# Sorted block attention into four weighted experts: the experts' weights of two chunks are spread over the partitions by GpSimd instead of by transfers, with 69 first dummy matmuls instead of 84

## The chip, the core and the metric

The kernel runs on one core of a Trainium2 chip. The metric is the device time of one execution in microseconds (us). Engines: PE multiplies matrices (PEld is its weight load), DVE is the vector engine, ACT the scalar engine, POOL is GpSimd, SP only issues transfers (DMA).

## What is computed

For each of 4 x 8 heads an 8 x 8 matrix is normalized over rows and columns five times. It mixes the 8 blocks of 96 keys and of 96 values. Each block of 96 queries attends to the mixed block at its place. The heads' results side by side are 3072 tokens x of width 512, which go through four experts; each expert's result counts with a weight p that depends on the token and the expert:

```python
p = domain_probs / (domain_probs.sum(-1, keepdims=True) + 1e-09)
for e in range(E):                       # 4 experts
    h = np.maximum(x @ w1[e], 0.0)       # 512 -> 1024
    out += p[:, e:e + 1] * (h @ w2[e])   # 1024 -> 512
```

## The kernel before

The order of the instructions on each engine is the order in which the program is written (manual_schedule): nothing is moved by a scheduler. Each engine works through its own list; semaphores make it wait for others.

**Start.** SP fetches the 8 x 8 matrices (L77) and the domain probabilities (L170, L171). PE runs `warm(84)` (L307), 84 matmuls on a constant tile that nobody reads. ACT and DVE take turns in the five normalization rounds (L309 to L327); after the last one `sn` is spread out (L330) and PE begins its real work with L342. Between rounds, `spread_weights` (L244) computes p on DVE, one step at a time. When p is done, SP writes its first 32 partitions, which hold batch 0's tokens, to a DRAM tile `p_dram` laid out expert by token (L256), and the rest after that (L258).

**Batch 0's attention, then its chunks.** Attention of batch 0 is done by the `h_` functions, in small steps between which expert 0's first layer (`group0`, L704) and second layer (`second_layer0`, L741) are put. Tokens are then handled in chunks of 256, three in a batch. `chunk_first(b, c, es, ...)` (L805) computes for each expert e of `es` the hidden values h: 2 groups of 16 matmuls (L815) into a PSUM tile of which there are two, and for each group one DVE instruction (L821) that takes max(h, 0), times the token's weight p for that expert, into `Hb`. Since tokens lie along the free axis there, p has to lie in the same row in all 128 partitions. That is what the tile `pb` is: 4 experts x 256 tokens, the same in each partition. Batch 0's expert 0 is handled otherwise, so its chunks need experts 1 to 3 only. `pb` has one buffer; the next chunk's weights can be written when the last L821 of the chunk is done.

**How pb is filled.** `load_p` (L226) is one transfer on SP's queue that reads a row of `p_dram` and writes it to all 128 partitions (512 KB for four experts). It is called for chunk (0, 0) right after L256 (L257), and for every next chunk in `chunk` (L847, L851). `load_p_one` (L238) fetches one expert's row of chunk (0, 1), 128 KB, into a part of tile `Tt[3]` (named T in the profile), for expert 1 of that chunk, which is computed early (call at L1506, use at L1516).

**POOL's list** holds all weight transfers (their descriptors are made by POOL: 0.7 to 0.9 us an issue), and its order matters here: `load_w1(1)`, the halves of `w1` of expert 2 (L1456), `load_w2(1)` and `load_w2(2)` (both issued at L146), `load_w1(3)` (L139), half of expert 3's `w2` (L1475), then four products that build mixing matrices for batch 1 (L372, L364 in `builds(1)`), then batch 1's queries (L126), values and keys (L113) with the other half of expert 3's `w2` among them. Before each issue POOL waits until the transfer that was issued eight before has landed.

**A chunk's second layer** (`chunk`, L834) is a sum of products of half blocks (a Strassen-like scheme). For chunk (0, 0) the steps are f1 (L950), f2 (L955), f3 and so on; between them some adds are POOL's (`gtt`: L953, L970, L971, L974, L995). POOL's list also has the query transfers of the next batch in between (L126). SP's list there: a transpose of queries (L413), pb of the next chunk (L230), six transfers of mixed values (L405), stores of the result (L876), more transposes.

**The end.** The last chunks (`last_first`, `last_second`) multiply again in seven products instead of eight (L1153, L1296); there POOL multiplies by p in L1166, 48 times in the last three pairs of chunks.

Of the kernel before, what the change touches and what calls it, by code (L numbers as in the profile page):

```python
# [2 lines left out]

# [7 lines left out]
F32 = mybir.dt.float32  # L11
# [7 lines left out]
def kernel(  # L19
# [11 lines left out]
    nc = tc.nc  # L31

    B, H, S, D = q.shape
# [4 lines left out]
    E = moe_w1.shape[0]  # L38
    FF = moe_w1.shape[2]
    P = 128  # L40
# [22 lines left out]
    moe = ctx.enter_context(tc.tile_pool(name="moe", bufs=2))  # L63
# [8 lines left out]
    def psm(shape, dtype, name):  # L72
        return psM.tile(shape, dtype, tag="ps", name=name)
# [46 lines left out]
    def load_queries(b, heads=range(H)):  # L120

        if (b, "q") not in natural:
            natural[(b, "q")] = arena[:, ds(4 * NW, NQ)].rearrange("p (n t h d) -> p n t h d", n=NPB, t=R, h=2)
        t = natural[(b, "q")]
        for h in heads:
            nc.gpsimd.dma_start(t[:, h // 2, :, h % 2, :], q[b, h].rearrange("(t p) d -> p t d", p=P))  # L126
# [16 lines left out]
    def load_w2(e, parts=1):  # L143
        n = NFC // parts
        for i in range(parts):
            nc.gpsimd.dma_start(  # L146
                w2sb[e][:, ds(i * n, n)], moe_w2[e].rearrange("(fc p) d -> p fc d", p=P)[:, ds(i * n, n)]
            )
# [71 lines left out]
    p_dram = dramp.tile([E, N], F32, name="p_dram")  # L220
# [2 lines left out]

    pbs = {}

    def load_p(b, c, es=range(E), pb=None):  # L226
        if pb is None:
            pb = moe.tile([P, E, 2 * P], F32, name=f"pb_{b}_{c}", tag="pb", bufs=1)
        n = len(es)
        nc.sync.dma_start(  # L230
            pb[:, ds(es[0], n)],
            p_dram[ds(es[0], n), ds(b * S + 2 * c * P, 2 * P)].rearrange("(o e) x -> o e x", o=1).broadcast_to(
                [P, n, 2 * P]
            ),
        )
        return pb

    def load_p_one(b, c, e):  # L238

        pb = Tt[3].rearrange("p a f x -> p (a f x)")[:, 0:4 * P].bitcast(F32)  # L240
        nc.sync.dma_start(pb, p_dram[ds(e, 1), ds(b * S + 2 * c * P, 2 * P)].broadcast_to([P, 2 * P]))
        return pb

    def spread_weights():  # L244

        nc.vector.tensor_reduce(p_den, p_in, AX.X, ALU.add)
        yield
        nc.vector.tensor_scalar(out=p_den, in0=p_den, scalar1=1e-9, scalar2=None, op0=ALU.add)
        yield
        nc.vector.reciprocal(p_den, p_den)  # L250
        yield
        nc.vector.tensor_tensor(
            p_out.rearrange("p e t -> p t e"), p_in, p_den.broadcast_to([P, NT, E]), ALU.mult
        )
        p_rows = p_dram.rearrange("e (p t) -> p e t", t=NT)
        nc.sync.dma_start(p_rows[0:S_P], p_out[0:S_P])  # L256
        pbs[(0, 0)] = load_p(0, 0)  # L257
        nc.sync.dma_start(p_rows[S_P:P], p_out[S_P:P])  # L258
        yield

# [11 lines left out]
    def warm(n):  # L272
        ps = psM.tile([P, 4, P], F32, tag="ps", name=f"ps_w_{state['n']}")
        state["n"] += 1
        for m in range(n):
            nc.tensor.matmul(ps[:, m % 4, :], dummy, dummy, start=True, stop=True)
# [27 lines left out]
    srow = const.tile([GH, NB, 1], F32, name="srow")  # L304
    scol = const.tile([GH, NB, 1], F32, name="scol")
    sn16 = const.tile([GH, NB, NB, CP], F16, name="sn16")
    warm(84)  # L307
    p_steps = spread_weights()
    for it in range(5):  # L309
        nc.scalar.activation(sn[:], sn[:], AF.Exp, bias=0.0, scale=1.0)  # L310
# [371 lines left out]
    def h0(fc):  # L682

        return Hflat[:, ds((0 if fc < KH else 3) * NFC * 2 * P + (fc % KH) * HS, HS)]
# [50 lines left out]
    def second_layer0(hf, slot):  # L735
        for t in range(R // 2):
            col = (R // 2) * hf + t
            po = psm([P, 2, 512], F32, f"ps_o_{col}")
            ps = po[:, 0, 0:Dm]
            for fc in range(NFC):  # L740
                nc.tensor.matmul(  # L741
                    ps, h0(fc)[:, ds(t * P, P)], w2sb[0][:, fc, :],
                    start=(fc == 0), stop=(fc == NFC - 1),
                )
                if fc == KH - 1:
                    slot()
            oaccs[col] = room[:, col - 2] if col > 1 else moeo.tile([P, Dm], F32, name=f"oacc_{col}", tag="oacc")
            nc.vector.tensor_scalar(
                out=oaccs[col][:], in0=ps, scalar1=p_sb[:, col], scalar2=None, op0=ALU.mult
            )  # L750
            slot()
# [53 lines left out]
    def chunk_first(b, c, es, first, slot, weights=None):  # L805

        xT = xTs[b].rearrange("p k i x -> p k (i x)")
        if weights is None:
            weights = lambda e: pbs[(b, c)][:, ds(e, 1), :]
        for e in es:  # L810
            for g in range(2):
                ps = psm([P, 4, 2 * P], F32, f"ps_h_{b}_{c}_{e}_{g}")
                for f in range(4):
                    for kc in range(NKC):
                        nc.tensor.matmul(  # L815
                            ps[:, f, :],
                            w1sb[e][:, kc, ds((4 * g + f) * P, P)],
                            xT[:, kc, ds(2 * c * P, 2 * P)],
                            start=(kc == 0), stop=(kc == NKC - 1),
                        )  # L820
                nc.vector.scalar_tensor_tensor(  # L821
                    out=Hb[:, homes.get(e, e), ds(4 * g, 4), :], in0=ps[:], scalar=0.0,
                    op0=ALU.max, in1=weights(e).broadcast_to([P, 4, 2 * P]), op1=ALU.mult,
                )
                late = e == E - 1 or b > c
                if e > first and (g or not late):
                    two = (2,) if b or c else (2, 3)
                    if b > c or (b, c, e) == (0, R // 2 - 1, E - 2):
                        two = ()
                    for w in (1, *two) if late else ((1,), two)[g]:  # L830
                        h_sums(e - 1, w)
                slot()

    def chunk(b, c, slot, done=()):  # L834

        es = list(range(E)) if b else list(range(1, E))
# [7 lines left out]
                h_sums(e, 2)  # L844
        nxt = (b, c + 1) if c + 1 < R // 2 else (b + 1, 0)
        first = int(nxt[0] == 0)
        pbs[nxt] = load_p(*nxt, range(first, first + 1))  # L847
        rest = lambda: load_p(*nxt, range(first + 1, E), pbs[nxt])
        late = b == c == 1
        if not late:  # L850
            rest()  # L851

        blk = lambda kh, tok: (lambda e, f: Hb[:, homes.get(e, e), kh * KH + f, ds(tok * P, P)])
        sm = lambda n: (lambda e, f: Sb[:, n, e, ds(f * P, P)])
# [1 line left out]
        def product(n, lhs, rhs, pool=psm):  # L856
            ps = pool([P, DH], F32, f"ps_{n}_{b}_{c}")
            for e in es:
                for f in range(KH):
                    nc.tensor.matmul(  # L860
                        ps[:], lhs(e, f), Ts[e][rhs][:, f, :],
                        start=(e == es[0] and f == 0), stop=(e == E - 1 and f == KH - 1),
                    )
            return ps[:]
# [7 lines left out]
        o = out[ds(b * S, S), :].rearrange("(t p) d -> p t d", p=P)  # L872
# [82 lines left out]
        def f2():  # L955
            tt(oa1, product("p2", blk(1, 0), "b21"), oa1, ALU.add)
            slot()
# [22 lines left out]
            h_sums(e, 4)  # L980
        next(steps)
        f2()
        next(steps)
        h_sums(E - 1, 3)
        f3()
# [483 lines left out]
            build_PI(nc.gpsimd, n, "k")  # L1469

    load_w2(1)
    load_w2(2)
    load_w1(3)
    def load_w2_part(e, d):
# [22 lines left out]
                f(*args)  # L1497

    second_layer0(0, next_stages)
    load_queries(1, range(2))  # L1500
    load_natural(1, "v", 0, 2, lambda: load_w2_part(3, DH))
    load_natural(1, "k", 0, 2)
    load_natural(1, "v", 1)
    load_natural(1, "k", 1)
    chunk_first(0, 0, [1, 2], 1, next_stages)
    pb_1 = load_p_one(0, 1, 1)  # L1506
    h_sums(1, 4)
    for w in range(1, 5):
        h_sums(2, w)
# [3 lines left out]
    second_layer0(1, lambda: next(sums2, None))  # L1513
    sums0 = weight_sums(0, nc.vector)
    homes[1] = 0
    chunk_first(0, 1, [1], 1, next_stages, lambda e: pb_1.rearrange("p (o x) -> p o x", o=1))  # L1516
    homes.clear()


    for g in range(G0 + 1):  # L1520
        b, c = divmod(g, R // 2)
# [5 lines left out]
        def slot(b=b, c=c, at=at):  # L1527
            here = (c, at[0])
            for cc, n, f, *args in PLANS[b]:
                if (cc, n) == here:  # L1530
                    f(*args)
            if b:
                for cc, n, *args in PLAN_A:
                    if (cc, n) == here:
                        input_sums(*args)
                if here == (1, 12):
                    token_sums(G0, slice(0, 3))
                if here == (2, 0):
                    token_sums(G0, slice(3, 4))
            at[0] += 1  # L1540
# [6 lines left out]
    for g in range(G0 + 1, GN, 2):  # L1547
        last_second(g, last_first(g))
        last_second(g + 1, upper=True)
# [1 line left out]
_INS = ['q', 'k', 'v', 'sort_net', 'moe_domain_probs', 'moe_w1', 'moe_w2']  # L1551
_OUTS = [((3072, 512), 'float32')]
# [25 lines left out]
```

## Time and profile before

| | |
|---|---|
| three runs | 358.37, 358.61, 359.99 us (median 358.61) |
| the profiled execution | 358.21 us |
| its span, first to last instruction | 356.3 us |
| PE busy | 350.4 us (98%) |
| DVE, ACT, POOL busy | 277.5, 170.1, 137.6 us |
| PE's granted clock | 1.0 throughout |

A line of a timeline reads: start in us, duration in us, engine, line of the kernel, operation, written tile <- read tiles, shape, count, and in brackets how long the engine was idle just before and what ended that. A line of the waits reads: engine and line that waited <- engine and line waited for: us in total, times, longest. In the list of transfers the last number of a line is the median of the us from issue to landing. In a table by stretches (start:end in us) the columns are the length of the stretch, then busy us and count by engine, the clock of PE, the share of the DMA engines, GB/s.

### The profile page before, as it was taken

Reading aid. Unit: us, or ns where it says so; the run is one execution under the profiler, and the core shown is the slowest. Engines: PE = TensorE matmul, PEld = TensorE weight load, DVE = VectorE, ACT = ScalarE, POOL = GpSimd, SP = SyncE. Lnnn points to the kernel's source line nnn. Section 1 sums busy time; section 2 is a strip of 40 time slices with the busy share of each in tenths; the row PEclk is TensorE's granted clock in tenths of the full one; section 3 lists DMA queues with packets and bytes.
Section 4 is the critical chain, followed back from the end, with each engine's and each line's share of the span. In section 5 each row is a group of like instructions: output and inputs, shape, how many; then the busy total and the mean of one; then the engine's idle time right before and its main releaser. Section 6 shows DMA issues by size and latency. Waiting matters only on the chain.

```text
span 356.3 us, 9511 instructions
## 1 busy us (share of the span) xinstructions
PE 350.4 (98%) x3948; PEld 305.5 (86%) x3948; DVE 277.5 (78%) x555; ACT 170.1 (48%) x302; POOL 137.6 (39%) x154
## 2 busy tenths in 40 slices
PE   8899999999999999999999999999999999999996
PEld 8686857888888888988899888888888888888886
DVE  5766787779798687778879988896678886588963
ACT  2653330452425445368847259830288611598301
POOL 8766112466022420000626318840068800188400
PEclk9999999999999999999999999999999999999999
DMA  8999999999999999743995410005200014100021
GB/s 104 203 205 230 212 209 194 207 195 167 195 180 166 195 116 203 138 88 44 180 205 91 107 74 0 2 1 136 78 26 3 2 37 141 62 0 2 0 75 46
DMA packets 74762, 40.26 MB, mean 113 GB/s; under 512 B 41568, under 2 KB 70496, under 8 KB 74720
## 3 DMA queue, kind: packets, MB, share of 16 engines
q0 software_dynamic: 38720, 19.93, 43.2%
q1 hardware_dynamic: 35856, 19.67, 27.2%
q8 instruction: 31, 0.51, 0.6%
q14 instruction: 11, 0.09, 0.1%
q10 hardware_dynamic: 144, 0.07, 0.1%
HBM read 41.88 MB, written 6.34 MB: 135 GB/s over the span
## 4 chain that ended last, share of the span: by engine, by line
PE 95%; DVE 3%; issue 0%; DMA 0%; ACT 0%; DVEq 0%
PE ps_h L815 18%; PE ps_Q L1296 18%; PE ps_p L799 12%; PE ps_X L1153 10%; PE ps_Z L1153 7%; PE ps_Q L1153 7%; PE ps_Z L1296 6%; PE ps_h L704 3%; PE ps_o L741 3%; PE ps_p L860 3%; PE ps_a L479 2%; PE ps_s L444 2%; PE ps_k L425 1%; PE ps_v L391 1%; PE ps_mv L521 1%; PE ps_a L593 0%
## 5 line engine op out<-in xcount | busy, mean ns | idle before, releaser
L815 PE MATMUL ps_h<-xT,w 128*128 128x256 f16 x576 | 67.5, 273 | 0.0
L815 PEld LDWEIGHTS <-w 128*128 128x128 f16 x576 | 55.2, 98 | 7.3
L821 DVE SCALAR_TENSOR_TENSOR Hb<-ps_h,pb 128x1024 f16<-128x1024 f32 x34 | 41.5, 1223 | 17.8 <-PE ps_h L815 17.6
L1153 PEld LDWEIGHTS <-w 128*128 128x128 f16 x480 | 43.6, 98 | 4.7
L1166 POOL TENSOR_TENSOR arena<-tmp,pb 128x512 f16<-128x512 f32 x12 | 15.2, 1276 | 65.7 <-PE ps_Z L1153 49.8
L1296 PEld LDWEIGHTS <-Hb 128*128 128x128 f16 x320 | 31.1, 98 | 3.5
L1165 ACT ACTIVATE tmp<-tmp 128x512 f32<-128x512 f32 x46 | 29.0, 632 | 3.9 <-DVE tmp L1203 3.9
L1296 PEld LDWEIGHTS <-Sb 128*128 128x128 f16 x304 | 28.2, 98 | 3.0
L1153 PEld LDWEIGHTS <-arena 128*128 128x128 f16 x312 | 27.7, 98 | 2.8
L451 ACT ACTIVATE ET<-ps_s 96x768 f16<-96x768 f32 x24 | 18.1, 802 | 25.2 <-PE ps_s L444 25.0
L434 ACT CAST kT<-ps_k 64x384 f16<-64x384 f32 x48 | 22.7, 473 | 13.3 <-PE ps_k L425 12.3
L126 POOL DMA_DIRECT2D arena<-in_q_dram x24 | 19.9, 842 | 20.8 <-DMA q_ring<-arena 17.7
L1153 PE MATMUL ps_X<-ET,arena 128*128 128x256 f16 x168 | 25.2, 272 | 0.0
L1296 PE MATMUL ps_Q<-w,Hb 128*128 128x256 f16 x192 | 24.6, 273 | 0.0
L799 PEld LDWEIGHTS <-Hb 128*128 128x128 f16 x232 | 21.9, 98 | 3.0
L1159 DVE SCALAR_TENSOR_TENSOR Hb<-ps_X,pb 128x512 f16<-128x512 f32 x27 | 18.7, 692 | 7.0 <-PE ps_X L1153 7.0
L1173 ACT COPY ps_X<-ps_Z 128x512 f32<-128x512 f32 x27 | 15.4, 571 | 17.8 <-PE ps_Z L1153 17.8
L1153 PE MATMUL ps_Z<-xT,w 128*128 128x256 f16 (+1 forms) x176 | 22.5, 258 | 0.0
L785 DVE TENSOR_TENSOR Sb<-Hb 128x512 f16<-128x512 f16 x33 | 20.6, 646 | 0.0
L1180 ACT COPY tmp<-ps_X 128x512 f32<-128x512 f32 x26 | 15.2, 586 | 9.2 <-PE ps_X L1153 6.6
L1159 DVE SCALAR_TENSOR_TENSOR Hb<-ps_Z,pb 128x512 f16<-128x512 f32 x27 | 18.4, 683 | 1.3 <-PE ps_Z L1153 1.3
L1203 DVE TENSOR_TENSOR tmp<-ps_Q,tmp 128x512 f32<-128x512 f32 x26 | 17.7, 683 | 0.8 <-PE ps_Q L1153 0.8
(270 smaller groups left out, 744.3 us busy)
## 6 DMA issues: line engine op xcount, KB each, us to landing
w<-in_moe_w_dram POOLq DMA_DIRECT2D x4, 1024.0 KB, 27.2
w<-in_moe_w_dram POOLq DMA_DIRECT2D x6, 512.0 KB, 19.7
arena<-in_k_dram POOLq DMA_DIRECT2D x7, 384.0 KB, 7.6
arena<-in_v_dram POOLq DMA_DIRECT2D x7, 384.0 KB, 8.1
vs<-arena SPq DMA_DIRECT2D x36, 66.0 KB, 5.3
arena<-in_q_dram POOLq DMA_DIRECT2D x24, 96.0 KB, 7.5
out_dram<-ob SPq DMA_DIRECT2D x9, 256.0 KB, 2.0
pb<-p_dram SPq DMA_DIRECT2D x4, 512.0 KB, 5.8
```

Source lines behind the costliest of these rows:

```text
L126: nc.gpsimd.dma_start(t[:, h // 2, :, h % 2, :], q[b, h].rearrange("(t p) d -> p t d", p=P))
L434: nc.scalar.copy(kT[ds(D * hh, D), r], pk[ds(D * r, D), hh].rearrange("p a (i c) -> p a i c", c=CP),)
L451: nc.scalar.activation(ETs[2 * (pr % 2) + hh][:, 0:S].rearrange("c (a x) -> c a x", a=2), pss[hh][0:BLK, :, 0:HS], AF.Exp, bias=0.0, scale ...
L785: tt(sm[0], blk(0, 1), blk(1, 1), ALU.add)
L799: nc.tensor.matmul(ps, lhs(e, f), Ts[e][rhs][:, f, :], start=(first and e == es[0] and f == 0), stop=(done and e == es[-1] and f == KH - 1 ...
L815: nc.tensor.matmul(ps[:, f, :], w1sb[e][:, kc, ds((4 * g + f) * P, P)], xT[:, kc, ds(2 * c * P, 2 * P)], start=(kc == 0), stop=(kc == NKC ...
L821: nc.vector.scalar_tensor_tensor(out=Hb[:, homes.get(e, e), ds(4 * g, 4), :], in0=ps[:], scalar=0.0, op0=ALU.max, in1=weights(e).broadcast ...
L1153: nc.tensor.matmul(dst[:, ds(f * cols, cols)], a[lhs][:, k, ds((f0 + f) * P, P)], t[rhs][:, k, :], start=(first and f == 0 and k == 0), st ...
L1159: nc.vector.scalar_tensor_tensor(out=home(i, j), in0=src.rearrange("p (f x) -> p f x", f=m), scalar=0.0, op0=ALU.max, in1=weight(j).broadc ...
L1165: nc.scalar.activation(src, src, AF.Relu, bias=0.0, scale=1.0)
L1203: tt(t12, Q, u2, ALU.add)
L1296: nc.tensor.matmul(ps, lhs(e, f), Ts[e][rhs][:, f, part], start=(first and e == 0 and f == 0), stop=(e == E - 1 and f == KH - 1), skip_gro ...
```

## The change

Three uses of transfers that write the same row to 128 partitions are replaced: chunk (0, 0), expert 1 of chunk (0, 1), and experts 2 and 3 of chunk (0, 1). Now a small transfer brings the rows to partition 0 (`load_rows`), and a GpSimd instruction copies partition 0 to all partitions (`spread`). [...] The row for `pb_1` is fetched and spread earlier in the lists than its transfer was: ahead of batch 1's query loads on POOL. The spread for chunk (0, 1) stands after f2 of chunk (0, 0) in the program, on POOL between L953 and the query loads. All other chunks use `load_p` as before. On PE, DVE and ACT nothing is moved; only 15 dummy matmuls with their weight loads are gone.

```diff
+    def pb_tile(b, c):
+        return moe.tile([P, E, 2 * P], F32, name=f"pb_{b}_{c}", tag="pb", bufs=1)
...
     def load_p_one(b, c, e):
         pb = Tt[3].rearrange("p a f x -> p (a f x)")[:, 0:4 * P].bitcast(F32)
-        nc.sync.dma_start(pb, p_dram[ds(e, 1), ds(b * S + 2 * c * P, 2 * P)].broadcast_to([P, 2 * P]))
+        pb = pb.rearrange("p (o x) -> p o x", o=1)
+        load_rows(pb, b, c, [e])
+        spread(pb)
         return pb
+
+    def load_rows(dst, b, c, es):
+        nc.sync.dma_start(
+            dst[0:1], p_dram[ds(es[0], len(es)), ds(b * S + 2 * c * P, 2 * P)].rearrange("(o e) x -> o e x", o=1)
+        )
+
+    def spread(dst):
+        nc.gpsimd.partition_broadcast(dst, dst[0:1])
...
         nc.sync.dma_start(p_rows[0:S_P], p_out[0:S_P])
-        pbs[(0, 0)] = load_p(0, 0)
+        pbs[(0, 0)] = pb_tile(0, 0)
+        load_rows(pbs[(0, 0)][:, 1:E], 0, 0, range(1, E))
         nc.sync.dma_start(p_rows[S_P:P], p_out[S_P:P])
...
-    warm(84)
+    warm(69)
...
-        pbs[nxt] = load_p(*nxt, range(first, first + 1))
-        rest = lambda: load_p(*nxt, range(first + 1, E), pbs[nxt])
         late = b == c == 1
-        if not late:
-            rest()
+        if nxt == (0, 1):
+            pbs[nxt] = pb_tile(*nxt)
+            load_rows(pbs[nxt][:, 2:E], *nxt, range(2, E))
+        else:
+            pbs[nxt] = load_p(*nxt, range(first, first + 1))
+            rest = lambda: load_p(*nxt, range(first + 1, E), pbs[nxt])
+            if not late:
+                rest()
...
         next(steps)
         f2()
+        spread(pbs[nxt][:, 2:E])
         next(steps)
...
     load_w2(1)
+    nc.gpsimd.load_library(library_config.all_libraries[10])
+    spread(pbs[(0, 0)][:, 1:E])
     load_w2(2)
...
     second_layer0(0, next_stages)
+    pb_1 = load_p_one(0, 1, 1)
     load_queries(1, range(2))
...
     chunk_first(0, 0, [1, 2], 1, next_stages)
-    pb_1 = load_p_one(0, 1, 1)
...
+    nc.gpsimd.load_library(library_config.standard)
```

More of the change, by code (lines that the diff above doesn't have):

```diff
@@ L5 @@
 import concourse.tile as tile
-from concourse import mybir
+from concourse import library_config, mybir
 from concourse.bass import ds
@@ L224 @@
     pbs = {}
+    def pb_tile(b, c):
+        return moe.tile([P, E, 2 * P], F32, name=f"pb_{b}_{c}", tag="pb", bufs=1)
     def load_p(b, c, es=range(E), pb=None):
         if pb is None:
-            pb = moe.tile([P, E, 2 * P], F32, name=f"pb_{b}_{c}", tag="pb", bufs=1)
+            pb = pb_tile(b, c)
         n = len(es)
@@ L1515 @@
     homes[1] = 0
-    chunk_first(0, 1, [1], 1, next_stages, lambda e: pb_1.rearrange("p (o x) -> p o x", o=1))
+    chunk_first(0, 1, [1], 1, next_stages, lambda e: pb_1)
     homes.clear()
```

## The prediction

> **What bounds the kernel now.** I read the page first (busy shares, then the chain that ended last), then the waits of TensorE alone, then POOL's and DVE's timelines around the changed lines, then the time to landing of the transfers issued there. Page:
>
> ```profile
> span 356.3 us, 9511 instructions
> ...
> PE 350.4 (98%) x3948; PEld 305.5 (86%) x3948; DVE 277.5 (78%) x555; ACT 170.1 (48%) x302; POOL 137.6 (39%) x154
> ...
> PE 95%; DVE 3%; issue 0%; DMA 0%; ACT 0%; DVEq 0%
> ```
>
> TensorE is on the chain for 95% of the span, DMA and POOL for nothing. A busy share alone could hide a PE that crawls, so the waits of the weight loads (PEld) over the whole run count more. Two of their lines:
>
> ```profile
> PEld L342 <- DVE sn L330: 1.4, 1, 1.4
> ...
> PEld L391 <- DMA arena<-in_v_dram: 0.2, 1, 0.2
> ```
>
> The first is the wait at 11.6 us for the end of the Sinkhorn rounds on ACT and DVE, which no edit touches. The second is all the time in the trace that PE waited for a transfer: 0.2 us. So whatever the change does to DMA, it has about 0.2 us to win in this trace, and the question is what it can break. What it touches, on POOL and DVE:
>
> ```profile
> 21.71 1.76 POOL L146 DMA_DIRECT2D w<-in_moe_w_dram  x2 [0.38 <-DMA w<-in_moe_w_dram]
> 23.50 0.75 POOL L139 DMA_DIRECT2D w<-in_moe_w_dram  x1
> 26.10 0.89 POOL L1475 DMA_DIRECT2D w<-in_moe_w_dram  x1 [1.86 <-DMA w<-in_moe_w_dram]
> 27.00 1.06 POOL L372 TENSOR_TENSOR arena<-maskv,Rs 128x512 f16<-128x512 f16 x1
> ...
> 40.88 0.90 POOL L1475 DMA_DIRECT2D w<-in_moe_w_dram  x1 [1.71 <-DMA w<-in_moe_w_dram]
> 47.35 0.70 POOL L113 DMA_DIRECT2D arena<-in_v_dram  x1 [5.58 <-DMA w<-in_moe_w_dram]
> ...
> 64.33 0.96 POOL L953 TENSOR_TENSOR oacc<-oacc,p 128x256 f32<-128x256 f32 x1 [2.83 <-ACT p L951]
> 65.25 1.69 POOL L126 DMA_DIRECT2D arena<-in_q_dram  x2
> 70.01 0.72 POOL L970 TENSOR_TENSOR oacc<-oacc,p 128x256 f32<-128x256 f32 x1 [3.07 <-ACT p L968]
> ```
>
> ```profile
> 38.79 1.23 DVE L821 SCALAR_TENSOR_TENSOR Hb<-ps_h,pb 128x1024 f16<-128x1024 f32 x1 [1.63 <-PE ps_h L815]
> ```
>
> ```profile
> pb<-p_dram SPq DMA_DIRECT2D x1, 512.0 KB, 10.4
> ...
> T<-p_dram SPq DMA_DIRECT2D x1, 128.0 KB, 12.6
> p_dram<-T SPq DMA_DIRECT2D x1, 36.0 KB, 12.2
> ```
>
> L821 at 38.79 us is the first reader of the spread weights; it waited for PE, not for them. The last fence is SP's transfers issued between 25 and 27 us, with the time to landing at the end of the line: the stretch is full of weight traffic, and even 36 KB took 12.2 us.
>
> **The change part by part.** All sums are made against the profiled execution: 358.2 us, span 356.3 and 1.9 around it. The median of the three runs, 358.6, lies 0.4 above it.
>
> *15 dummies fewer.* The first dummies by time, columns PE busy and count:
>
> ```profile
> 1.06:3.06 2.00, 2.00 (x19) 0.00 (x0) 1.00 0.16 31
> 3.06:5.06 2.00, 2.00 (x21) 0.00 (x0) 1.00 1.15 133
> 5.06:7.06 2.00, 2.00 (x39) 0.00 (x0) 1.00 1.17 127
> ```
>
> 105 ns each for the first 19, 51 ns in the third stretch. The 15 last cost 15 x 0.051 = 0.8 us, and the first 69 end near 6.5 us, after the speed doubled. PE then waits longer before L342 (1.2 us on its own row becomes 2.0): 0 on the path. If that cover were gone it would be a gain of at most 0.8.
>
> *Transfers removed.* 512 KB and 128 KB near 26 us, and 384 KB at 63.8 us, become rows of 3, 1 and 2 KB. The DMA moves 211 to 227 GB/s between 20 and 40 us, so 640 KB less lets the weights behind land about 3.0 us earlier. PE's wait for v goes: -0.2. Next is k at L425, which landed at 66.8 and is taken at 67.0; it would be early by the same 3 us. If the stream were not relieved (the change not doing what it says), this 0.2 alone is lost: 358.5.
>
> *Library load and first spread on POOL.* They stand between the two issues of L146, so POOL reaches them at 22.6. The trace has no real load. From below: the two configuration instructions of masks.py:199, 0.09 us each. [...] I take 10.4, the 512 KB transfer: the load ends at 33.0. The row of 3 KB is issued at 25.5 and lands in 1.5 (sn, 8 KB, idle DMA) to 12.2 us (36 KB); I take 5.5, the 12 KB write issued at 20.0: 31.0. The spread of 768 elements is 0.3 (a COPY of 128) to 1.9 us (1.28 of a TENSOR_TENSOR of 512 f32, times 1.5); I take 1.9. Done at 34.9, or 39.6 by the latest row; L821 wants it at 38.79, and PE goes on behind it, because its next group has a second PSUM buffer. Cost 0, slack 3.9.
>
> Behind the load on POOL wait three weight issues (2.5 us: to 37.4), four builds (4.1: 41.5), the second, smaller spread (0.6: 42.1; its reader L821 comes at 57.4), two query issues (43.8), v (44.5) and w2's second half, at 44.5 instead of 40.88. What hides it: the software queue holds a backlog. The w2 part issued at 21.71 landed 25.1 us later, at 46.8; the next only has to be in the queue by about 43.8 (3.0 us earlier than that landing), and it is at 34.9. At 47.35 POOL waited 5.58 us for a landing anyway, so there it is in step again. Without that backlog it would cost the whole 12 us.
>
> *Third spread.* On POOL after L953, waiting for a row issued at 63.8. Bounds 1.5 and 7.0 (128 KB there); 5.5 gives 69.3, the spread of 512 ends at 70.6, its reader L821 comes at 75.1. Queued behind it: two query issues (to 72.3 instead of 66.9), L970 and L971 (73.7), L995 (74.4), L974 (75.3), four query issues from 75.3 instead of 73.6. The first two queries landed after 10.7 us behind a backlog (76.8); issued late they take the 4.9 us of those issued at 70 to 75: 76.3, no later. The next two come 1.7 us later, and with them SP's queue: transposes, six vs transfers, the weights of the third chunk (85.2 to 86.9, 7.7 to landing: 94.6). Their L821 stands at 94.11, so DVE is 0.5 late; PE's third group there starts at 96.5 and needs that L821's end, 95.8. Cost 0.
>
> *Library at the end.* POOL's last TENSOR_TENSOR ends at 333.8 and PE's last matmul at 353.5: a load of 12.6 fits. 0.
>
> To cover the small slips in this I add 0.3: 358.2 - 0.2 + 0.3 = **358.3**.
>
> [...]
>
> **Rivals.**
> 1. *The load is slow; the kernel gets slower.* It decides from 14.3 us (22.6 + 14.3 + 1.9 = 38.8). For it: weights of 512 KB took 19.7 us to land (median of the six), and POOL can do nothing else meanwhile. Against it: SP's queue stayed under 12.7. At 19.7 the spread ends at 44.2, L821 at 45.4; PE's third group, at 41.1, waits 4.3: **362.5**.
> 2. *POOL is held at the third spread.* Decides from 6.8 us of landing: then the two queries pass 77.7, and PE's L444 at 86.08, whose operand landed at 85.2, waits. At 8.6 (the 256 KB there) 1.8 us: 360.0; at 12.2 about 5. Against it: two kilobytes.
> 3. *The new library's tensor_tensor is slower.* L1166 takes 1.27 us, twice in each step of 3.06 us. Up to 1.53 nothing is lost; at twice the time each of 24 steps loses 2.0: 407. The trace has no word for it.
> 4. *The clock drops in the longer wait at 11.6.* Half speed for 3.4 us would cost at most 1.7: 359.9. Against it: PEclk shows full clock, and 1.2 us of waiting did no harm. [...]
> 5. *Faster.* Unprofiled runs may wait for landings more than this trace does (one took 360.0). To pass 0.5% the gain must be 1.8 us, nine times the wait seen: 356.7.
>
> **Chances.** Forecast 0.52; slow load 0.20; third spread 0.13 (0.05 of it small); tensor_tensor 0.04; clock 0.03 (0.02 small); faster 0.08. Of a measurement of this kernel, 0.5% (1.8 us: 356.8 to 360.4) is about what can be told from no change. So faster 0.08, same 0.52 + 0.05 + 0.02 = 0.59, slower 0.20 + 0.08 + 0.04 + 0.01 = 0.33. The range runs from 357.4 (most of the gain left out) to 362.5 (slow load in, tensor_tensor and the worst rows out): about 0.8.
>
> **What would show it.** Right: PE's waits as before, without the one on v; POOL's spread before 38 us; L821 there still released by PE; the weights about 3 us earlier. Wrong: L821 released by POOL at 38.8 (rival 1); L444 near 86 waiting for q_ring (rival 2); L1166 far from 1.27 us (rival 3); matmuls after 11.6 at twice their length (rival 4). The forecast falls with any PE wait over 1.8 us that is not in the trace of before.

## The result, and the profile after

| | before | changed |
|---|---|---|
| median of 22 runs each | 358.37 us | 359.16 us |
| lowest to highest | 357.86 to 359.99 | 357.98 to 361.91 |
| ratio, 95% interval | | 1.0024 (1.0014 to 1.0034) |
| profiled execution, its span | 358.21, 356.3 | 360.12, 358.2 |

The changed kernel is 0.8 us (0.24%) slower. That is inside the range (357.4 to 362.5) and within the 0.5% that was called "same", but it is not the 0 that the sum gave: the interval leaves 1.0 out. The whole of it has to be explained by small things, so the experiments below count in tenths of a per cent.

In this kernel 14 lines were added ahead of the attention code: L821, L413, L405, L342, L479, L495 and L815 of before are L835, L427, L419, L356, L493, L509 and L829 here, and L230 is L233. The page of the changed kernel, its span, its busy shares and the shares of the chain by engine:

```profile
span 358.2 us, 9489 instructions
...
PE 350.7 (98%) x3933; PEld 305.5 (85%) x3933; DVE 277.3 (77%) x555; ACT 170.1 (47%) x302; POOL 139.8 (39%) x157
...
PE 87%; DMA 5%; DVE 5%; SPq 1%; issue 1%; ACT 0%; DVEq 0%
```

The busy shares say nothing: PE still has 98%. The chain does: DMA and SP's queue now hold 6% of it, where they held nothing. The waits of TensorE (engine and line that waited <- engine and line waited for: us in total, times, longest) tell where:

```profile
PE ps_R L356 <- DVE sn L344: 1.2, 1, 1.2
...
PE ps_a L493 <- DMA vs<-arena: 0.6, 1, 0.6
PE ps_h L829 <- DVE Hb L835: 0.6, 1, 0.6
PE ps_h L829 <- DMA xT<-xsl: 0.4, 1, 0.4
```

The last three are new. They stand at 97.0, 117.3 and 125.7 us, where PE stands idle for 0.60, 0.42 and 0.64 us: 1.66 together, of 1.9 us more span. POOL's timeline shows the spreads (start, duration, engine, line, operation, [idle before and what ended it]):

```profile
21.96 0.88 POOL L146 DMA_DIRECT2D w<-in_moe_w_dram  x1 [0.35 <-DMA w<-in_moe_w_dram]
30.94 1.05 POOL L255 PARTITION_BROADCAST pb<-pb  x1 [8.09 <-DMA pb<-p_dram]
31.85 1.07 POOL L146 DMA_DIRECT2D w<-in_moe_w_dram  x1
...
38.62 0.55 POOL L255 PARTITION_BROADCAST T<-T  x1
```

```profile
69.48 0.80 POOL L255 PARTITION_BROADCAST pb<-pb  x1 [4.37 <-DMA pb<-p_dram]
70.12 1.73 POOL L126 DMA_DIRECT2D arena<-in_q_dram  x2
...
74.80 3.30 POOL L126 DMA_DIRECT2D arena<-in_q_dram  x4
```

The load of library 10 (L1491) and the row together held POOL 8.09 us; by the profile the row came last, so the load took no longer than that. Behind it POOL runs both the spread (L255) and TENSOR_TENSOR (L386, 1.09 us at 34.57; 1.06 at L372 before). The first spread is over at 32.0, and its reader L835 at 38.61 waits for no weights. At the third spread POOL stood 4.37 us for a row of two kilobytes. DVE's timeline around the first of the new waits, of before and of the changed kernel:

```profile
94.11 1.23 DVE L821 SCALAR_TENSOR_TENSOR Hb<-ps_h,pb 128x1024 f16<-128x1024 f32 x1 [0.26 <-PE ps_h L815]
```

```profile
95.76 2.36 DVE L835 SCALAR_TENSOR_TENSOR Hb<-ps_h,pb 128x1024 f16<-128x1024 f32 x2 [2.18 <-DMA pb<-p_dram]
```

DVE waited for the third chunk's weights and began 1.65 us later than in the profile before, and PE for DVE. Those weights still come by a transfer (L233); nothing of the change touches them directly. And one thing the profile does not show at all, since this execution ran at full clock: in 14 of the 22 runs PE's mean granted clock was below 1.0 (seven at 0.995, six at 0.99, one at 0.985). So there are two causes to look for: a clock and a late transfer.

### The profile page after: what moved, and what is told of

It is laid out like the page before. It is cut to its first block, busy times and chain, and to the rows that moved or that the text cites. A ratio compares the mean times of both kernels' runs of the same rounds, so it can differ in the third digit from the quotient of the medians.

```text
span 358.2 us, 9489 instructions
## 1 busy us (share of the span) xinstructions
PE 350.7 (98%) x3933; PEld 305.5 (85%) x3933; DVE 277.3 (77%) x555; ACT 170.1 (47%) x302; POOL 139.8 (39%) x157
## 3 DMA queue, kind: packets, MB, share of 16 engines
q1 hardware_dynamic: 34780, 18.62, 26.9%
## 4 chain that ended last, share of the span: by engine, by line
PE 87%; DMA 5%; DVE 5%; SPq 1%; issue 1%; ACT 0%; DVEq 0%
PE ps_Q L1315 18%; PE ps_h L829 15%; PE ps_X L1172 10%; PE ps_p L813 9%; PE ps_Z L1172 7%; PE ps_Q L1172 7%; PE ps_Z L1315 6%; PE ps_o L755 3%; PE ps_h L718 3%; PE ps_p L878 3%; DMA pb<-p_dram 3%; DMA vs<-arena 2%; PE ps_a L493 1%; PE ps_v L405 1%; PE ps_s L458 1%; SPq L419 1%
## 5 line engine op out<-in xcount | busy, mean ns | idle before, releaser
L829 PE MATMUL ps_h<-xT,w 128*128 128x256 f16 x576 | 67.7, 273 | 1.0 <-DVE Hb L835 0.6
L829 PEld LDWEIGHTS <-w 128*128 128x128 f16 x576 | 55.2, 98 | 8.6 <-issue 1.3
L835 DVE SCALAR_TENSOR_TENSOR Hb<-ps_h,pb 128x1024 f16<-128x1024 f32 x34 | 41.5, 1223 | 20.0 <-PE ps_h L829 14.6
L1185 POOL TENSOR_TENSOR arena<-tmp,pb 128x512 f16<-128x512 f32 x12 | 15.2, 1276 | 65.7 <-PE ps_Z L1172 49.8
L1049 POOL DMA_DIRECT2D arena<-w x4 | 4.9, 1451 | 34.6 <-PE ps_a L493 33.0
```

Source lines behind the costliest of these rows:

```text
L829: nc.tensor.matmul(ps[:, f, :], w1sb[e][:, kc, ds((4 * g + f) * P, P)], xT[:, kc, ds(2 * c * P, 2 * P)], start=(kc == 0), stop=(kc == NKC ...
L835: nc.vector.scalar_tensor_tensor(out=Hb[:, homes.get(e, e), ds(4 * g, 4), :], in0=ps[:], scalar=0.0, op0=ALU.max, in1=weights(e).broadcast ...
```

## The experiments

Every median below is of 12 runs unless it says otherwise, beside 23 to 35 runs of the kernel before on the same chip. Over the five batches these are 151 runs with a median of 358.35, 18 of them at 359 or over, 8 below clock 0.998.

### The clock: the number of first dummies alone

The kernel before with 69 first dummies, and nothing else:

```diff
-    warm(84)
+    warm(69)
```

> The kernel before with 69 first dummies and nothing else. Clock theory (the shorter warm-up leaves PE idle longer before 11.6 us, and in part of the executions the granted clock drops for one or two stretches of some 3.4 us): all of the loss is here, +0.6 to +0.9 us (ratio 1.0016 to 1.0025), with runs whose mean clock is 0.995 or 0.99. Third-spread theory (POOL held at the third spread makes SP's transfers late): no difference, under 0.15 us, clock 1.0.

Measured: 359.03 (357.99 to 360.63), ratio 1.0013 (0.9992 to 1.0034). The interval is wide because the runs fall into groups by clock: three at 0.999 with 357.99 to 358.30, four at 0.995 with 358.83 to 359.05, four at 0.99 with 359.66 to 359.89, one at 0.986 with 360.63. Each step down in the clock is 0.8 us. The dose was doubled, `warm(54)`:

> The kernel before with 54 first dummies. Clock theory: idle time before 11.6 us longer again, so the clock drops in more than the 9 of 12 runs of e1_dummies69, median +0.7 to +1.8 us, and a profile with a stretch of PEclk below 9 early in the run. Rival (the number does not matter, e1 was chance): same as before.

Measured: 360.55 (7 runs), ratio 1.0049 (1.0031 to 1.0066), every run at 0.985 to 0.995. By the ratio that is 1.8 us over before, the upper end of what was expected, by the medians 2.2. Its profile, in stretches (start:end, length, then busy us and count of PE, PEld, DVE, ACT, POOL, then PE's clock, DMA share, GB/s):

```profile
9.00:10.00 1.00, 0.00 (x0) 0.00 (x0) 0.82 (x5) 0.38 (x2) 0.84 (x4) 1.00 1.26 190
10.00:11.00 1.00, 0.00 (x0) 0.00 (x0) 0.90 (x4) 1.00 (x2) 0.94 (x10) 1.00 1.34 202
11.00:12.00 1.00, 0.00 (x0) 0.00 (x0) 0.93 (x3) 0.24 (x1) 0.81 (x4) 0.96 1.21 184
12.00:13.00 1.00, 0.94 (x12) 0.90 (x12) 0.54 (x3) 0.00 (x0) 1.00 (x2) 0.50 1.32 199
13.00:15.00 2.00, 2.00 (x59) 1.70 (x59) 0.43 (x2) 0.49 (x2) 1.90 (x3) 0.50 1.31 205
...
18.00:19.00 1.00, 1.00 (x34) 0.82 (x29) 0.35 (x1) 0.69 (x1) 0.99 (x2) 0.62 1.30 221
```

PE did nothing for three stretches; then, as its real work began at 12 us, it ran at half clock. From the shares 0.96 and 0.62 the half clock lasts from 11.92 to 18.76, 6.84 us. Half of that lost out of 358 is a mean clock of 0.990, which is the group "0.99"; a group at 0.995 has had 3.4 us of it.

Is it the idle time or the number of first dummies? Fifteen dummies back, but in the second set, which fills the idle time:

```diff
-    warm(84)
+    warm(69)
...
-            warm(30)
+            warm(45)
```

> The kernel before with 69 first dummies and 45 instead of 30 in the second row of dummies, so as many in all as before, and PE idle no longer before 11.6 us. Theory 'the idle time before 11.6 us drops the clock': same as the kernel before (within 0.15 us), mean clock 1.0 or 0.999. Rival 'the first dummies must be long enough for the speed to come': as e1_dummies69, +0.7 us, most runs at 0.995 or 0.99.

Measured: 358.49, 1.0003 (0.9992 to 1.0015), all twelve at 0.999 or 1.0. It is the idle time ahead of L342. That this idle time differs from execution to execution is seen in the dummies themselves: the time at which they double their speed is 5.04 us in the profile before, 6.97 in the changed kernel's, and from 4.03 to 6.73 in those of the first eight experiments. An early doubling ends the dummies early and makes the wait long. In the profile of the 69 alone it doubled at 4.0, and the wait was 3.0 us, not 2.0. That execution kept its clock all the same (0.999, 358.30 us), so a long wait alone doesn't make the loss.

A second place showed a drop in an experiment made for another purpose (the hold of 9.9 us, below). Its PE waited from 97.25 to 100.22 us in the middle of the kernel, in all four runs the clock was 0.995, and the profile has:

```profile
97.00:100.00 3.00, 0.25 (x5) 0.13 (x3) 1.06 (x1) 1.89 (x4) 0.00 (x0) 0.93 1.73 210
100.00:103.00 3.00, 2.78 (x14) 1.92 (x14) 1.30 (x2) 0.00 (x0) 0.00 (x0) 0.50 1.78 128
103.00:106.00 3.00, 3.00 (x41) 2.73 (x40) 2.31 (x3) 0.00 (x0) 0.43 (x1) 1.00 1.22 267
```

From the share 0.93 the half clock begins at 99.58, which is 2.3 us after the last matmul and before the wait was over. The clock records of the profiles tell when it changes. In the four profiles with a drop, the clock was full for 6.83, 10.24, 10.24 and 95.57 us, counted from the doubling to the drop, and then half for 6.83, 6.83, 3.41 and 3.41; in the 15 others that have such records it was full for 351.57. All of these are whole multiples of 3.413 us: 2, 3, 3 and 28 times, 2, 2, 1 and 1, and 103 times. So in these 19 profiles the clock changed on a grid of 3.413 us that begins at the doubling; since the doubling moves by some 3 us, the same wait falls on it differently from execution to execution. PE's busy share in the step of the grid just ahead of the drop was 0.06, 0.58, 0.60 and 0.32; but a step of 0.47 (the 69 alone) and one of 0.58 (69 with the third spread later, below) did no harm, so this share alone does not decide, and what does stays open.

A long wait is not needed for a drop: it came 2.3 us into the wait here, and in one run below (the changed kernel with 69 and 45) after a wait of 1.8 us, while the wait of 3.0 us with the 69 alone did no harm. So a wait shorter than 3 us can cost the clock.

### The spreads: where the rest comes from

The changed kernel with `warm(84)`, so that only the spreads are left:

> The changed kernel with 84 first dummies again, so the spreads alone. Clock theory: within 0.2 us of the kernel before, mean clock 1.0 in nearly all runs. Third-spread theory: +0.6 to +0.9 us, and the trace has PE waits near 97 us (L829 for L835) and at 117 to 126 us that sum to 1 to 2 us.

Measured: 359.04 (358.0 to 360.56), 1.001 (0.9991 to 1.0028), all at full clock. So the spreads cost time of their own. Twice more, once the same and once as the changed kernel with `warm(45)` as its second set:

> The changed kernel with 84 first dummies again, as in the run that gave 359.04 with an interval that still held 1.0 (0.9991 to 1.0028), to narrow it. Theory 'the spreads cost time of their own, beside the dummies': median 358.8 to 359.2, ratio 1.001 to 1.003, all executions at full granted clock. Rival 'the spreads cost nothing, and the 359.04 was scatter': 358.2 to 358.5, ratio within 0.9995 to 1.0008.

> The changed kernel with one edit: the second set of dummies 45 instead of 30. Theory 'the changed kernel's 0.8 us are mostly the dropped clock': no execution below clock 0.999 but rare ones, and 358.5 to 358.9, like the spreads with 84 first dummies. Rival 'the clock has little to do with it': 359.1 to 359.3 as the changed kernel, with the clock at 0.99 to 0.995 in more than half of the executions.

Measured: 358.74 (1.0002, 0.9989 to 1.0015) and 359.01 (1.0018, 1.0006 to 1.003). The first of these alone would not have told 0 from 0.4 us. The clock was below 0.999 in one run of each. The run of the 69 and 45 that has a profile is one of them: PE waited 1.8 us ahead of L356, its matmuls paused again for 0.4 us (13:14 below), and half clock followed at 14.15, 2.5 us after the end of that wait.

```profile
11.00:12.00 1.00, 0.35 (x7) 0.33 (x8) 0.59 (x1) 0.00 (x0) 1.00 (x10) 1.00 1.33 212
12.00:13.00 1.00, 0.96 (x41) 0.89 (x41) 0.75 (x2) 0.00 (x0) 1.00 (x2) 1.00 1.30 197
13.00:14.00 1.00, 0.59 (x31) 0.47 (x25) 0.52 (x1) 0.48 (x1) 0.77 (x2) 1.00 1.30 200
14.00:15.00 1.00, 1.00 (x15) 0.88 (x14) 0.04 (x1) 0.70 (x2) 0.00 (x0) 0.57 1.28 203
```

Which spread? The second chunk's experts 2 and 3 by transfers again (no third spread), and, in another kernel, the third spread moved behind f5, where POOL's first adds are done and the first two queries are out (both with `warm(84)`):

```diff
         f2()
-        spread(pbs[nxt][:, 2:E])
...
         f5()
+        spread(pbs[nxt][:, 2:E])
```

> 84 dummies, the library load and the first two spreads; chunk (0, 1)'s experts 2 and 3 by transfers as before. Clock theory: same as e2_spreads84, 0 to 0.2 us over the kernel before. Third-spread theory: the loss of e2_spreads84 is gone, within 0.2 us of the kernel before, no PE wait near 97 us. If the library load or the first spread cost something, it shows here.

> 84 dummies, all three spreads, the third one behind f5 instead of f2: on POOL it then stands after the query loads and the two adds that follow, when its row has landed, so that POOL is not held. Clock theory: same as e2_spreads84. Third-spread theory: 0 to 0.3 us over the kernel before, query loads issued near 65 us again, no PE wait near 97 us.

Measured: without it 358.66 (1.0007, 0.9988 to 1.0026), which is unclear; behind f5 358.25 (0.9992, 0.9976 to 1.0008). Once more, and with the dummies as 69 and 45:

> All three spreads with 84 dummies, the third one behind f5, once more: 358.25 before, without one execution over 358.8. Theory 'behind f5 the spreads cost nothing': 358.1 to 358.4, at most one execution in ten at 359 or over. Rival 'the first result was a lucky dozen, the spreads cost wherever they stand': 358.6 to 359.0, a quarter or more at 359 or over.

> The third spread behind f5, and the dummies as 69 and 45 (15 moved from the first set to the second; that change alone on the kernel before gave 358.50). Theory 'both losses gone': 358.1 to 358.5, all executions at granted clock 0.999 or 1.0. Rival 'the idle time before L342 also lets PE's instructions run ahead, and without it PE finds gaps of issue (84 and 45 gave 360.02, with 1.5 us of them)': 358.6 or more at full clock.

Measured: 358.21 (1.0005, 0.9992 to 1.0017) and 358.24 (11 runs; 1.0002, 0.9993 to 1.0011). The place of the third spread is what matters; the load and the first two spreads, which these versions keep, cost nothing that the runs can tell. The changed kernel with only this move keeps the clock's loss:

> The changed kernel with its 69 dummies, but the third spread behind f5 as in e4_third_later. If the two losses come from two causes and one hides the other in the changed kernel: the clock's loss alone, +0.5 to +0.8 us, runs at 0.995 and 0.99 and no late run at clock 1.0. If the third spread were the whole loss of the changed kernel: as e4_third_later, 358.3.

Measured: 358.71 (1.0011, 0.9995 to 1.0026); seven runs at full clock (median 358.15, one of them at 358.98, where no late one was expected), five below it (358.82 to 360.81).

Is it the spread at that place, or POOL's wait for the row? In the next kernel the spread stays behind f2, but its rows are fetched some 20 us earlier, into partition 0 of `sn16`, which nobody reads any more:

```diff
     second_layer0(0, next_stages)
+    p_row23 = sn16.rearrange("g a b c -> g (a b c)").bitcast(F32).rearrange("g (e x) -> g e x", e=2)
+    load_rows(p_row23, 0, 1, range(2, E))
...
-            load_rows(pbs[nxt][:, 2:E], *nxt, range(2, E))
...
-        spread(pbs[nxt][:, 2:E])
+        spread(pbs[nxt][:, 2:E], p_row23[0:1])
```

> All three spreads with 84 dummies, the third one at its place behind f2, but its rows fetched some 20 us earlier into partition 0 of a tile that is free by then (sn16): POOL doesn't wait for a landing there, the spread follows L953's successor at once, and the first two query loads go out at about 66 instead of 69.5 to 70. Theory 'the wait for the row is what costs in the version with the spread there (358.74 and 359.04)': 358.2 to 358.5, few executions at 359 or over. Rival 'it is the spread itself or the freed transfers, not the wait': 358.7 to 359.1 with a third or more of the executions at 359 or over.

Measured: 358.25 (11 runs, 357.77 to 359.06; 0.9997, 0.9989 to 1.0006). Its POOL:

```profile
65.54 0.97 POOL L255 PARTITION_BROADCAST pb<-sn  x1
66.35 1.73 POOL L126 DMA_DIRECT2D arena<-in_q_dram  x2
```

The spread stands at the same place; only the wait is gone. With `warm(84)` or 69 and 45, the three series with the wait (36 runs) together have a median of 358.92 and 16 runs at 359 or over, the four without it (46 runs) 358.25 and 5. The difference is 0.7 us (0.4 to 0.9 by resampling the runs).

### Is it the hold of POOL?

POOL held by memsets that nobody reads, at the same place: on the kernel before, with 4.9 us (twice) and 9.9 us; on the version with the late spread 4.9, on that with the early row 3.9.

```diff
         f2()
+        for _ in range(5):
+            nc.gpsimd.memset(sn16[:], 0.0)
```

> The kernel before, with 5 memsets of a tile that is no longer used on POOL at the place of the third spread (some 4.4 us), no library, no spread, weights by transfers. Theory 'the loss of the spreads is POOL being held there': +0.4 to +0.8 us with a wide scatter like e2_spreads84. Rival 'it is the library or the broadcast itself': same as before.

> The kernel before with five unused memsets on POOL (4.9 us, queries at 71.2) once more: 358.38 the first time, 3 of 12 executions at 359 or over. Theory 'lateness of the queries costs also without the freed transfers': 358.6 or more. Rival 'with the transfers of the kernel before, 4.9 us are still covered': 358.2 to 358.45.

> The kernel before with ten instead of five unused memsets on POOL behind L953: POOL is held for about 9.9 us, to 76, and the first two query loads go out at about 76 instead of 65.3 (with five memsets 71.2), the four others at about 81 instead of 73.6. Theory 'the hold alone makes the queries late and that is what the third spread costs': the two first queries land about 5 us later than with five memsets, SP's transposes and the weights of the third chunk follow, and PE waits from 86 us on: 361 to 363, ratio 1.008 or more. Rival 'there is slack for it, and what the third spread costs is not its hold': within 0.2% of before (358.3 to 359.0).

> All three spreads with 84 dummies, the third one moved behind f5 (that version took 358.25), and five unused memsets on POOL at the place from which it was moved: POOL is held 4.9 us there with no row to wait for, and the queries go out at about 71 instead of 65.3. Theory 'it is the hold, together with the transfers that the spreads free, that costs': 358.8 to 359.3, like the version with the spread there. Rival 'it is the row's transfer or the spread itself at that place, not the hold': 358.2 to 358.5.

> The version whose third row is fetched early (358.25), with four unused memsets behind the third spread: POOL is held about 3.9 us with no transfer to wait for, and the first two query loads go out at about 70.3, where the versions that wait for the row send them (69.4 to 70.7, pooled 358.92). Theory 'lateness of the queries is what costs, whatever makes them late': 358.7 to 359.1, a third or more of the executions at 359 or over. Rival 'a wait for a transfer costs something that a hold of the same length does not': 358.2 to 358.4.

Measured: on the kernel before 358.38 (1.0005, 0.9993 to 1.0017) and 358.64 (1.0001, 0.9991 to 1.0011), 363.72 for 9.9 us (4 runs; 1.0142, 1.0121 to 1.0162). With the spreads 358.61 (0.9998, 0.9983 to 1.0013) and 358.75 (1.0009, 0.9993 to 1.0024); these two together (24 runs) lie 0.5 us over the versions without a hold (0.0 to 0.6), 0.3 (-0.2 to 0.5) when each run is taken against the kernel before of its own batch. So it is not shown that a hold with no transfer to wait for costs what the wait costs: the rival, that the wait for a transfer does something that a hold of the same length does not, stays open. On the kernel before the same hold costs 0.1 (-0.1 to 0.4), and twice as long a hold costs 5, more than expected. That is the shape of a cliff, not of a price per us.

### What lies at the edge of the cliff

All 20 profiles show it (this is read from runs already made, not foretold). Behind the held queries on SP's queue stands the second transpose of queries (L427). Near 80 us POOL issues the next values and keys (L113), 384 KB each, when PE releases a buffer. Of the changed kernel, POOL and SP in that stretch:

```profile
79.57 0.74 POOL L113 DMA_DIRECT2D arena<-in_v_dram  x1 [0.72 <-PE ps_v L405]
80.30 0.76 POOL L113 DMA_DIRECT2D arena<-in_k_dram  x1
```

```profile
80.88 1.22 SPq L427 DMA_TRANSPOSE q_ring<-arena  x1
```

The same of the version with the early row:

```profile
80.03 0.74 POOL L113 DMA_DIRECT2D arena<-in_v_dram  x1 [2.17 <-PE ps_v L405]
```

```profile
79.89 1.21 SPq L427 DMA_TRANSPOSE q_ring<-arena  x1
```

and what the transpose took from issue to landing in the one and in the other (lists of the transfers issued from 79 to 81.3 us):

```profile
q_ring<-arena SPq DMA_TRANSPOSE x1, 10.6
```

```profile
q_ring<-arena SPq DMA_TRANSPOSE x1, 5.2
```

| second transpose issued | profiles | issue to landing |
|---|---|---|
| ahead of that value load | 11: before, 69, 54, 69 and 45, no third spread, third later (3 of 4), early row, 84 and 45, hold 4.9 on before (second) | 3.9 to 7.6 us |
| behind it | 9: changed, spreads with 84 (both), changed with 69 and 45, third later with 69, holds of 4.9 (first), 9.9, and both holds with the spreads | 9.1 to 10.8 us |

The two groups don't touch. In six of the nine only the value load went ahead of the transpose, and the key load came after it, so one load of 384 KB is enough. The margin is small: 0.51 us in the profile before, 0.14 with the early row; the same kernel (hold of 4.9) fell on either side in two profiles, and the third spread behind f5 once fell behind the load although its queries were issued at 65.1 us. What comes after it is in SP's queue, of the changed kernel and then of before:

```profile
76.32 5.78 SPq L427 DMA_TRANSPOSE q_ring<-arena  x2
82.19 4.14 SPq L419 DMA_DIRECT2D vs<-arena  x6
86.43 5.46 SPq L233 DMA_DIRECT2D pb<-p_dram  x2
92.42 1.24 SPq L509 DMA_TRANSPOSE xT<-xsl  x1
```

```profile
76.82 3.73 SPq L413 DMA_TRANSPOSE q_ring<-arena  x2
80.64 4.46 SPq L405 DMA_DIRECT2D vs<-arena  x6
85.22 1.35 SPq L230 DMA_DIRECT2D pb<-p_dram  x2
88.52 1.25 SPq L495 DMA_TRANSPOSE xT<-xsl  x1
```

The transfers on SP's queue land in the order in which they are issued (in all 20 profiles, from 60 to 130 us), so all that stand behind the late transpose land late. The pair of weight transfers is one of expert 1 (128 KB) and one of experts 2 and 3 (256 KB). The first was issued at 86.43, before the transpose had landed, and landed at 95.67, after 9.2 us where before it took 7.7. That is what DVE's L835 waited for. Its piece of the chain that ended last:

```profile
86.43 9.23 DMA pb<-p_dram
```

The second was issued only at 91.52, because SP waited for the transpose to land (91.50):

```profile
SPq L233 <- DMA q_ring<-arena: 4.5, 1, 4.5
```

No DVE instruction waited for it, but everything behind it on SP's queue is 4 us late, L509 among it. That the waits at 117.3 and 125.7 us come from there fits the order of the queue; no run tested it.

The edge alone is not the loss. All 20 profiles can be compared from the end of DVE's sixth L821 (63.79 us in the profile before) on:

| landing of expert 1's weights after the sixth L821 | profiles | from the sixth to the 13th L821 |
|---|---|---|
| 26.9 to 29.8 us | the 11 with the transpose ahead | 35.84 to 35.97 us |
| 30.5 to 31.3 us | spreads with 84 (first), changed with 69 and 45, hold of 4.9 (first), early row with hold | 35.84 |
| 31.5 us | spreads with 84 (second), third later with hold | 36.08, 36.06 |
| 31.9 us | third later with 69 | 36.43 |
| 32.1 us | changed | 36.60 |
| 35.0 us | hold of 9.9 | 40.92 |

With the transpose behind the value load the weights land 30.5 us or more after the sixth L821, ahead of it 29.8 or less. The loss begins at about 31.3, and from there to 32.1 each tenth of a us of landing is a tenth of a us of time. The profile before has 2.2 us of slack there. So the late transpose uses up most of a slack, and only some executions pass its end. Of the nine behind the load, four lose nothing from the sixth to the last L821 (121.7 us, as the eleven ahead of it), and the others 0.2, 0.6, 1.0, 2.1 (the changed kernel, whose profile is the slowest of its runs at full clock) and 5.1 us. All other differences between the profiles lie ahead of 64 us.

The order is shown in 20 profiles, and the versions with early row and with the hold behind it move it as intended (one edit, ahead; the other, behind). That the value load is what the transpose then waits for inside the DMA is argued from the order alone; no run took these loads away.

### A version that fills all the idle time

> Candidate that keeps the full clock and the early queries: all three spreads, 84 first dummies, the second set of dummies 45 instead of 30 (so that PE hardly idles before L342), the third spread behind f5. Theory 'the losses were the dropped clock and the held queries, and the freed transfers are worth nothing or a little': 358.0 to 358.3, all executions at clock 0.999 or 1.0, ratio 0.998 to 1.000. Rival 'the spreads cost something wherever they stand': 358.6 or more.

Measured: 360.02 (11 runs, 1.0042, 1.0026 to 1.0058), nine of the eleven at full clock, these from 359.49 to 360.53; the expectation was wrong. L356 starts at 11.69 as in the version without the 15 added dummies, so PE was not late. The waits of TensorE show what was not there before:

```profile
PE ps_a L607 <- issue: 0.6, 1, 0.6
PE ps_w L562 <- issue: 0.5, 1, 0.5
PE ps_mv L535 <- issue: 0.4, 1, 0.4
```

"issue" is time in which PE waited for nothing that the profile shows; it is 1.5 us of a loss of 1.7. It stands at 13.6, 19.8 and 32.0 us, behind a stretch in which PE had hardly any idle time (0.3 us ahead of L356, 1.6 without the dummies). That the missing idle time causes these gaps is not shown: in five other profiles PE has a gap of issue of 0.4 to 0.7 us ahead of L342 (L356) near 14 us, with 0.3 to 1.8 us of idle time before the real work (both holds of 4.9 on before, 69 and 45, changed with 69 and 45, early row with hold). What PE's issue lacked, instructions or something else, stays open.

None of the versions beats the kernel before by more than the runs can tell; the lowest ratios are 0.9992 (third spread later; 1.0005 the second time) and 0.9997 (early row).

## Why the prediction was right and wrong

**What held.** The load was done by 30.9 instead of 33.0 (8.09 us with the wait for the row, 10.4 taken); the row came at 30.9 (31.0 taken); the spread of 768 took 1.05 (1.9 taken), that of 512 0.80 (1.28), that of 256 0.55 (0.6). What the load took alone is hidden behind the row, and no run shows it; nor does one show the 10.4 and the 12.6 that stood for a load in the sums, or that a load is a transfer: the two queues of instructions moved 0.51 and 0.09 MB in the profile before and in the changed kernel's. The weights behind landed 3.0 us earlier, as said (51.9 became 48.8, 64.4 became 61.4), and the wait on v is gone. The backlog covered POOL's delay: PE has no new wait before 97 us. The second library does not change tensor_tensor (L1166, now L1185: 1.27 us in both), so rival 3 falls, and with the early spread rival 1.

**"15 dummies fewer ... 0 on the path": failed, by the size of a wait.** "1.2 us on its own row becomes 2.0" took the time of the speed's doubling from one profile (5.04). It moves by some 3 us between executions, and with it the end of the dummies, the length of the wait (1.2, 1.4 and 3.0 us in the three profiles with 69 and 30) and the grid on which the clock changes. In part of the executions the clock then halves for 3.4 or 6.8 us. None of these three caught such an execution, so how long their waits were isn't known; that the missing dummies ahead of L342 cause the drops is shown by the runs with 69, 54, and 69 and 45. That is rival 4, which had 0.03 with "1.2 us of waiting did no harm" as its reason; in 14 of 22 runs it came. Two profiles show its 3.4 us of half speed, 3.41 each (the hold of 9.9 us, the changed kernel with 69 and 45). Its price of at most 1.7 for that was right as a bound: 0.8 was measured, and 1.7 for two such stretches.

**"Third spread ... Cost 0": failed, at one step.** The row at 69.3 (69.48), the first two queries' landing at 76.3 (76.26), the SP queue's delay of 1.7 (1.5), and the issue of the third chunk's weights at 86.9 (86.43 for the first) were nearly right. Then the sum took "7.7 to landing" from before and let the queue go on as it was. The second transpose had slipped behind a value load of 384 KB (here a key load too) and landed 5.3 us later (91.50 instead of 86.18); the weights of expert 1 behind it on the queue took 9.2 us to landing and came at 95.67 instead of 94.6. L821's successor ended at 97.0 instead of 95.8, and PE's third group, wanted at 96.5, waited. The test named for rival 2, "L444 near 86 waiting for q_ring", did not fire: its start (POOL held, queries late) comes nearest to what happened, but the price is paid ten us further on, by weights and not by queries. With a hold of 9.9 us it is 363.7, about what rival 2 gave for its worst row.

**The sum of the two.** Singly, the spreads cost 0.6 (358.92 against 358.35) and the dummies 0.7 (359.03 against 358.35); together 0.8. So the two don't add. The eight runs of the changed kernel at full clock have a median of 358.95, the time of the spreads alone; six of the seven at clock 0.995 lie between 358.81 and 359.24 and the six at 0.99 between 359.63 and 359.86, the times of the 69 alone in the same groups. So an execution that lost its clock pays next to nothing for the spreads, with one exception (360.23 at 0.995). That a PE which is 0.8 us late meets the late transfers 0.8 us later would explain it, and is argued only. The gain of 0.2 is somewhere under this. The forecast "falls with any PE wait over 1.8 us that is not in the trace of before": no wait was that long; two causes of half that size were enough.

## What to carry to other kernels

When a step is moved by one or two us, don't shift the rest of the queue by that amount: look which transfers of other queues it now starts behind, since a 1.5 us slip past a load of 384 KB became 5 us. Then ask how much slack is left there: 2.2 us hid most of it, and only the executions that passed its end were slower. And an idle time taken from one profile is one draw: here PE's speed doubled anywhere between 4 and 7 us, so a margin against the clock has to hold for that whole range, not for the one in the trace. Where such effects overlap, test each alone before adding them up.

## What the hardware showed beyond that

- In the changed kernel's profile a GpSimd broadcast from one partition to 128 took 0.55, 0.80 and 1.05 us for 256, 512 and 768 f32 elements: 0.25 us for each 256 more. That of 512 took 0.80 to 0.97 us in eight other profiles, 1.23 and 1.29 in two.
- The load of the standard library at the end cost nothing that the runs can tell (358.2 to 358.3 in four series that have it).
- PE's clock changed only at whole multiples of 3.413 us after the doubling of its speed (19 profiles). Where it dropped, it was half for 3.41 or 6.83 us. It fell to half 2.3 us after the last matmul in the middle of the kernel, 3.2 us after it with 54 dummies, and 2.5 us after the end of a wait of 1.8 us in one run at the start; in another a wait of 3.0 us did no harm. What decides between these is open.
- The second transpose of queries, by DMA, landed after 3.9 to 7.6 us when it was issued ahead of the 384 KB value load of another queue (11 profiles), and after 9.1 to 10.8 us behind it (9).
- PE lost 1.5 us to three gaps of issue between 13.6 and 32.0 us in one profile, and 0.4 to 0.7 us in five others. What makes them is open.
